# Window attention and two expert layers on one core: fifteen lists of steps in place of fixed offsets, key maxima two head pairs at once, and lists for the first steps of layer two

## The chip, the cores and the metric

The kernel runs on one core of a Trainium2 chip. The metric is the device time of one execution in microseconds (us), as the median of several runs. A core has five engines with a queue of instructions each: TensorE (PE; the loading of its weights is listed apart as PEld), VectorE (DVE), ScalarE (ACT), GpSimd (POOL) and SyncE (SP), which here only issues transfers (DMA). An engine runs its own queue in order and waits for others by semaphores.

## The reference, cut to what matters

```python
def _attn_ref(q, k, v):                       # 2 batches, 8 heads, 768 x 64
    block, window = (32, 16)
    k_sum = k.reshape(B, H, nb, block, D).max(axis=3)      # 24 key maxima
    v_sum = v.reshape(B, H, nb, block, D).mean(axis=3)     # 24 value means
    scores_l = scale * q @ k.T, kept where |i - j| < window
    scores_s = scale * q @ k_sum.T + log(block)
    a = softmax(concat([scores_l, scores_s]))   # with 1e-9 added to the sum
    return a @ concat([v, v_sum])

def _moe_ref(x, w_in, w_out, alpha):          # x 1536 x 512, w_in 512 x 2048, w_out 2048 x 512
    h = x @ w_in
    return (max(h, 0) + alpha * min(h, 0)) @ w_out

def _moe2_ref(x, w_in, w_out, a, b):          # the same sizes
    h = x @ w_in
    P = a[0] + a[1]*h + a[2]*h**2 + a[3]*h**3
    Q = 1 + abs(b[0])*abs(h) + abs(b[1])*h**2
    return (P / (Q + 1e-6)) @ w_out

def reference(...):
    x = _attn_ref(q, k, v), as 1536 x 512
    return _moe2_ref(_moe_ref(x, ...), ...)
```

## The kernel before, in words

**Attention.** The 1536 queries are 24 tiles of 64, n = 0 to 23; a tile has all eight heads, as four pairs. Its steps, by the names in the lists of orders and the lines of the functions: `qk`, the scores on PE into the one PSUM bank s (L554); `mask`, mask, scale and row minimum on DVE (L563); `sub`, for some tiles, subtracts the minimum ahead of the exponential; `exp` on ACT (L575, L579); `sum` on DVE (L584) or `guard` on one of three engines (L592 to L596), which form the sum d; `inv`, its reciprocal on DVE (L600); `norm`, p times d on POOL (L604); `turn`, a transpose on PE (L610); `turned`, the copy pT of it on ACT (L205); `pv`, the products po with the values (L624); `out`, a cast of po to xh (L205 on ACT, L207 on others); `outl`, the rest xl = po - xh on DVE (L645). The string SOFTMAX has one letter for each tile: a, the exponential sums itself by an accumulator and `guard` adds 1e-9; b, DVE sums; s, the minimum is subtracted first and one exponential does all four pairs. A tile's keys are copied to one of two buffers kc: `k` the strip of 96 keys for each pair, `ks` the 24 key maxima. The maxima (L477) are DVE reductions of one head pair and one half of a batch, eight for each batch. The value means are products on PE (`vmean`, L498; vps), for the second batch of rows that DVE has added in pairs (`vadd`, L493), copied out by ACT (L503) and put beside a tile's values by `vm`.

**Layer one beside it.** Every product with a weight is three products: weight and activation are each a high half of few bits and a low rest (xh and xl, wih and wil, woh and wol, g's two), and only low times low is left out. A weight arrives as raw 64-bit words in pieces of 1 MB, in two buffers. A piece is made ready in steps: ACT takes the tops (L230), DVE joins them to cv (`low`, L232), a cast gives the high half (`hi`), and two subtractions of 128x512 give the low one (`mid`, `end`, L253). For the first 512 tokens layer one begins as soon as their tiles are there: H (L290), the activation on DVE (`act`, L309 and L315), the cast of g and its low part (`gh`, `gl`, L207 and L354), Y (L370), in halves of 256 tokens for the first eight chunks of the hidden width. H and Y are numbered here in the order in which they come: 0 to 23 are the 24 of the first 512 tokens in layer one, and H24 and Y24 are the first of layer two.

**What sets the order.** There is no scheduler: each engine's order is the order in which the code issues. Iteration t = -1 to 27 walks one of seven lists in ORDERS, chosen by PHASES, and each step in it works on tile t plus a fixed offset. Ten constants (VMEAN_AT to WLOAD_AT) say at which iteration the loads, means and maxima come, BUSY and WARM where products of the unit matrix on itself are put whose result nobody reads ("idle", L674). The strings ENG name the engine of a step by phase: v is DVE, a is ACT, p is POOL.

**After attention** come what is left of layer one for the first 512 tokens (BETWEEN), the other 1024 tokens in a scheme that saves one product in eight (PAIRED, L920 and L941), and layer two (DECODE). There each round of `run` (its loop is below) issues an H, then the steps of the weights in preparation, the parts of P and Q of earlier chunks, up to six steps left over from PAIRED, and at most two Y.

Of the kernel before, what the change touches and what calls it, by code (L numbers as in the profile page):

```python
# [22 lines left out]
P = 128  # L23
WINDOW = 16
# [7 lines left out]
START_H = 6  # L32
N_FIRST = 3
HALVES = 8
EARLY = 8

VMEAN_AT = (-1, -1, 0, 1, 1, 2)
VADD_AT = (11, 11, 11)
VLOAD_AT = (9, 9, 9)
VSUM_AT = 12  # L40
KMAX_AT = (8, 9, 10, 8, 10, 10, 10, 10)
KLOAD_AT = (6, 8)
WLOAD_AT = (1, 3)

PHASES = (3, 5, 7, 10, 14, 20)
ORDERS = (
    "qk exp end sum k turn act vm vadd turned mask gh hi sub pv vmean kmax v gl in act new out H guard low inv "
    "mid Y ks act outl norm",
    "act hi exp low qk in mid vm turn mask gh sum act pv k H vmean turned gl out ks vadd guard act inv new v outl "
    "sub norm kmax Y end",  # L50
    "vm qk exp act mask mid pv v sum gh guard act Y kmax k out hi outl gl vadd low inv in norm ks turn end turned "
    "vmean H act sub new",
    "vm gh new act pv vadd exp mid hi end gl qk act act out kmax in sum outl turn k mask Y v vmean low guard sub "
    "ks inv turned norm H",
    "gh act end exp act ks qk mid gl act hi pv v out mask sum in outl Y vadd new sub vm vmean turn kmax H k "
    "turned guard inv low norm",
    "act act kmax act vm qk mask exp gh Y end guard sum gl pv vadd hi mid out k turn outl sub vmean H inv v norm "
    "ks new turned in low",
    "vm act exp hi qk vadd act act in guard mask k pv out kmax v outl sum gh Y mid turn new gl inv ks norm end H "
    "low vmean sub turned",  # L60
)

FIRST = 'v1 k0 v0 k1 v2 q0 v3 q1'

SOFTMAX = 'aaabbbaaaaasbbabaababbba'

ENG = {"vadd": "v", "guard": "pvavavaaaaa", "k": "vavaaapvaaa", "turned": "aaaaaaaaaaa", "vm": "pppvpvapaaa",
       "ks": "ppppvvvaaaa", "norm": "ppppppppaaa", "sub": "vpvvvpvaaaa", "gl": "vpppvpvvpvv", "gh": "aaapapavaap",
       "hi": "vvvaaaaaaav", "mid": "pvpppvvppvv", "end": "ppppppvvppp", "out": "aaavavaaaaa", "E1": "a",
       "neg": "aavvvvvvvvv", "th": "aaaavaaaaaa", "tl": "vvpppvpvppp", "ta": "p", "tb": "p",  # L70
# [7 lines left out]
LEAD = (5, 7, 3, 4, 13, 14, 9, 15)  # L78
CLOSE_E = 9
# [6 lines left out]
X_AT = (3, 4, 6)  # L86
# [11 lines left out]
BETWEEN, PAIRED, DECODE = 7, 8, 9  # L98
START_ORDER = ("new end Y P2 end P1 P6 E1 end T3 late P5 end ms C11 hi t11 low t11 l22 P7 T2 h21 low low P3 "
               "late U2 U4 U3 C22 hs new t22 t11 end low P4 new end C12 C21 t22 Y l21 t12 t21 T1 hi t12 ms es "  # L100
               "ms h22 hi t22 late mid ms t21 t12 Y mid low mid h11 es l11 h12 Y t21 T0 l12 end").split()
# [14 lines left out]
def kernel(  # L116
# [356 lines left out]
    def att_kmax(b, i):  # L473
        half, hp = divmod(i, NPAIR)
# [65 lines left out]
    def att_ksum(n):  # L540
        b, j = divmod(n, NSUB)
        if j < NKC:
            copy("ks", kc[n % NKC][:, :, STRIP:KEYS], kmax[b])

    def att_k(n):
        b, j = divmod(n, NSUB)
        half, j = divmod(j, HSUB)
        copy("k", kc[n % NKC][:, :, 0:STRIP], kt[b, half][:, :, j * QS:j * QS + STRIP])

    def att_scores(n):  # L550
        j = n % NSUB
        s = ps_s.tile([P, NPAIR, KEYS], F32, tag="s", name="s")
        for hp in range(NPAIR):
            nc.tensor.matmul(out=s[:, hp, :], lhsT=qz[n % NQZ][:, hp, :], rhs=kc[n % NKC][:, hp, :],  # L554
                             start=True, stop=True)
        st[n] = s
# [110 lines left out]
    def keep_busy(t, step):  # L667
        unread(BUSY.get((t, step), 0))

# [39 lines left out]
    later = {}  # L709

    acts, split_at = [], {}

    def ff_y(t):
        if split_at.get(y_list[0], t) < t and (0, "wo", y_list[0][1] // 2) in wts:
            y_mm(*y_list.pop(0))

    def ff_h(t):
        u, f = h_list[0]
        if u[:2] == (0, 0) and ready(u) <= t and (0, "wi", f // 2) in wts and len(y_list) - len(h_list) < 3:
            h_list.pop(0)  # L720
            h_mm(u, f)
            acts.append(act1(u, f))
            later[t + 2] = u, f
            split_at[u, f] = t + 2

    def vmean_at(t):
        for i, at in enumerate(VMEAN_AT):
            if at == t:
                att_vmean(i)
        while vlate:  # L730
            att_vload(vlate.pop(0))
        for i, at in enumerate(VLOAD_AT):
            if at == t:
                att_vpair(i)
        if t == VSUM_AT:
            att_vsum()

    def vadd_at(t):
        for i, at in enumerate(VADD_AT):
            if at == t:  # L740
                att_vadd(i)

    def kmax_at(t):
        for i, at in enumerate(KMAX_AT):
            if at == t:
                att_kmax(1, i)
# [14 lines left out]
    def w_step(place, most=0, alone=False):  # L761
# [5 lines left out]
        if len(w_now) < most and preps and preps[0] in raws and now[0] > loaded[preps[0]] + (1 if now[0] <= LAST else 2 if "wo" in kept and not rest and st2 else 0):  # L767
# [5 lines left out]
    attn = {"vm": (att_vm, -3), "ks": (att_ksum, 1), "k": (att_k, 1), "exp": (att_exp, -1), "qk": (att_scores, 0),  # L773
            "mask": (att_mask, 0), "sum": (att_sum, -1), "sub": (att_shift, 0),
            "guard": (att_guard, -1), "inv": (att_inv, -1), "norm": (att_norm, -1), "pv": (att_pv, -3),
# [4 lines left out]
    with tc.manual_schedule():  # L780
        for step in FIRST.split():
            {"k": lambda i: att_load(0, i), "v": att_vload, "q": att_in}[step[0]](int(step[1]))
        for i in range(2 * NPAIR):
            att_kmax(0, i)
# [339 lines left out]
```

## Time and profile before

| | before |
|---|---|
| median of 3 runs | 604.16 us (603.86 to 604.42) |
| profiled execution | 603.79 us |
| its span | 602.1 us |
| PE busy | 589.0 us, 98% |
| DVE busy | 518.6 us, 86% |
| ACT busy | 357.2 us, 59% |
| POOL busy | 304.6 us, 51% |
| moved by DMA | 71.64 MB, mean 119 GB/s |

The span runs from the first to the last instruction of the profiled execution; 1.7 us of its time lie around it. Busy times are of one execution. In the timeline an instruction has its start and its duration, and in brackets, where its engine sat idle ahead of it, for how long and what it waited for. Durations of PE's products overlap, since one product is still running out while the next is begun; where two follow each other without a pause, the distance of their starts is what one costs.

### The profile page before, as it was taken

The page shows a single profiled execution, that of the slowest core. Times are in us where ns is not written, and L with a number is a line of the kernel's source. Part 1 is how long each engine was busy: PE and PEld are TensorE (multiplying, and loading weights), DVE is VectorE, ACT ScalarE, POOL GpSimd, SP SyncE. Part 2 cuts the span into 40 slices and gives each one's busy share as a digit, 9 for nine tenths or more (in the row PEclk, how much of TensorE's full clock was granted, in tenths as well). Part 3 has the DMA queues.
Part 4 walks back from the last instruction along what each step waited for, and adds up shares of the span by engine and source line. Part 5 has one row for each costly group of instructions (what it writes and reads, how often), then busy time and mean ns, then how long its engine had stood idle before and what let it go on. Part 6 is the DMA issues. An engine that isn't in the chain of part 4 may idle for free.

```text
span 602.1 us, 9108 instructions
## 1 busy us (share of the span) xinstructions
PE 589.0 (98%) x3212; PEld 491.2 (82%) x3212; DVE 518.6 (86%) x990; ACT 357.2 (59%) x614; POOL 304.6 (51%) x332
## 2 busy tenths in 40 slices
PE   8998999999999999999999999999999999999997
PEld 6787899887888888888888778888888888888885
DVE  4689999989989999999988899999877778677785
ACT  1787778566465545554546878886555554454442
POOL 4475577686343424422442865456545554355552
PEclk9999999999999999999999999999999999999999
DMA  9999768424431342524334333330100000100001
GB/s 298 320 306 319 253 233 276 150 71 142 153 127 70 121 142 88 209 83 144 124 118 162 140 139 109 110 133 0 71 1 1 0 1 0 72 0 1 1 2 70
DMA packets 18862, 71.64 MB, mean 119 GB/s; under 512 B 2560, under 2 KB 4608, under 8 KB 12672
## 3 DMA queue, kind: packets, MB, share of 16 engines
q1 hardware_dynamic: 18816, 71.06, 34.5%
q8 instruction: 25, 0.41, 0.3%
q14 instruction: 21, 0.17, 0.1%
HBM read 67.91 MB, written 3.15 MB: 118 GB/s over the span
## 4 chain that ended last, share of the span: by engine, by line
PE 84%; DVE 9%; ACT 3%; POOL 2%; issue 2%; POOLq 0%; ACTq 0%; DVEq 0%
PE y L370 27%; PE h L290 26%; PE h L920 13%; PE h L941 7%; PE y L941 6%; DVE cv L232 2%; PE s L554 2%; PE vps L498 1%; PE po L624 1%; DVE wol L253 1%; ACT p L579 1%; PE pt L610 1%; DVE p L563 1%; ACT top L230 1%; DVE g L354 1%
## 5 line engine op out<-in xcount | busy, mean ns | idle before, releaser
L370 PE MATMUL y<-woh,g 128*128 128x512 f32 x384 | 126.2, 391 | 1.2 <-DVE g L354 1.2
L290 PE MATMUL h<-xh,wih 128*128 128x512 f32 (+1 forms) x288 | 106.9, 371 | 1.9 <-DVE tu L315 1.6
L290 PE MATMUL h<-xl,wih 128*128 128x512 f32 (+1 forms) x288 | 105.3, 366 | 0.8 <-DVE xl L645 0.8
L290 PE MATMUL h<-xh,wil 128*128 128x512 f32 (+1 forms) x288 | 105.2, 365 | 0.0
L329 POOL TENSOR_SCALAR tu<-tv,ab 128x512 f32<-128x512 f32 x48 | 38.8, 809 | 114.8 <-ACT tv L327 114.8
L370 PEld LDWEIGHTS y<-woh,g 128*128 128x128 f32 x384 | 71.7, 188 | 17.4 <-DVE g L354 2.7
L338 ACT ACTIVATE h<-tu,lnb 128x512 f32<-128x512 f32 x47 | 32.6, 693 | 82.7 <-DVE tp L332 80.3
L370 PE MATMUL y<-wol,g 128*128 128x512 f32 x192 | 74.7, 389 | 0.0
L230 ACT ACTIVATE top<-raw 128x1024 f16<-128x1024 bf16 x48 | 66.3, 1382 | 5.0 <-issue 2.5
L330 POOL TENSOR_TENSOR tu<-tu,tv 128x512 f32<-128x512 f32 x48 | 62.3, 1298 | 4.0
L290 PEld LDWEIGHTS h<-xh,wih 128*128 128x128 f32 x288 | 54.2, 188 | 11.4 <-DVE tu L315 2.1
L290 PEld LDWEIGHTS h<-xl,wih 128*128 128x128 f32 x288 | 54.3, 188 | 9.7 <-DVE xl L645 1.0
L232 DVE SCALAR_TENSOR_TENSOR cv<-raw,top 128x1024 int32<-128x1024 int32 x48 | 59.9, 1248 | 1.8 <-ACT top L230 1.6
L290 PEld LDWEIGHTS h<-xh,wil 128*128 128x128 f32 x288 | 54.2, 188 | 8.8
L340 DVE SCALAR_TENSOR_TENSOR tu<-tu,h 128x512 f32<-128x512 f32 x47 | 32.2, 686 | 28.2 <-ACT h L339 28.0
L205 ACT ACTIVATE wih<-cv 128x1024 fp32r<-128x1024 f32 x31 | 32.5, 1052 | 27.4 <-DVE cv L232 27.4
L604 POOL TENSOR_TENSOR p<-p,d 128x480 f32<-128x480 f32 x24 | 31.2, 1301 | 32.2 <-DVE d L600 26.8
L997 DVE TENSOR_TENSOR e<-h,e 128x512 f32<-128x512 f32 x56 | 37.8, 688 | 9.4 <-PE h L920 7.5
L370 PE MATMUL y<-g,woh 128*128 128x256 f32 (+1 forms) x192 | 45.5, 328 | 0.2 <-DVE g L354 0.2
L1023 POOL TENSOR_TENSOR g<-tu,g 128x512 fp32r<-128x512 f32 x16 | 28.3, 1768 | 29.7 <-ACT g L205 29.0
L370 PEld LDWEIGHTS y<-wol,g 128*128 128x128 f32 x192 | 36.0, 188 | 7.6
L354 DVE TENSOR_TENSOR g<-tp,g 128x512 fp32r<-128x512 f32 (+1 forms) x55 | 38.3, 696 | 1.8 <-POOL g L207 1.6
(141 smaller groups left out, 1419.2 us busy)
## 6 DMA issues: line engine op xcount, KB each, us to landing
raw<-in_w_in SPq DMA_DIRECT2D x24, 1024.0 KB, 4.8
raw<-in_w_out SPq DMA_DIRECT2D x24, 1024.0 KB, 4.7
qz<-in_qT SPq DMA_DIRECT2D x24, 256.0 KB, 4.9
vc<-in_vS SPq DMA_DIRECT2D x24, 192.0 KB, 5.0
kt<-in_kT SPq DMA_DIRECT2D x16, 208.0 KB, 5.5
out<-stage SPq DMA_DIRECT2D x12, 256.0 KB, 2.3
vt<-in_vS SPq DMA_DIRECT2D x6, 256.0 KB, 4.4
vp<-in_vS SPq DMA_DIRECT2D x3, 512.0 KB, 8.0
```

The source lines that it names most:

```text
L205: e.activation(out=out, in_=in_, func=AF.Copy, scale=1.0 if scale is None else scale)
L230: nc.scalar.activation(out=top.bitcast(F16)[:, 1::2], in_=raw.bitcast(BF16)[:, 4:4100:4], func=AF.Copy)
L232: nc.vector.scalar_tensor_tensor(out=w.bitcast(I32), in0=rest, scalar=13, in1=top, op0=ALU.logical_shift_right, op1=ALU.bitwise_or)
L290: nc.tensor.matmul(out=ps, lhsT=a, rhs=b, start=(c == 0 and m == 0), stop=(c == NC - 1 and m == 2))
L329: nc.gpsimd.tensor_scalar(out=q, in0=v, scalar1=ab[:, 1:2], scalar2=ab[:, 0:1], op0=ALU.mult, op1=ALU.add)
L330: nc.gpsimd.tensor_tensor(out=q, in0=q, in1=v, op=ALU.mult)
L338: nc.scalar.activation(out=A, in_=q, func=AF.Ln, scale=2.0 ** -LN_SHIFT, bias=lnb)
L354: (eng("gl") if (u, f) != steps[-1] else nc.vector).tensor_tensor(out=gl, in0=t, in1=gh.bitcast(F32), op=ALU.subtract)
L370: nc.tensor.matmul(out=yps[c][:, c0:c0 + n] if layer == 0 else yps[c], lhsT=a, rhs=b, start=(f == 0 and c0 == 0 and m == 0), stop=(f == NF ...
L920: nc.tensor.matmul(out=ps, lhsT=a[:, cs], rhs=b, start=c == 0 and m == 0, stop=c == 1 and m == 2)
L941: nc.tensor.matmul(out=ps, lhsT=a[:, f, cs], rhs=g[:, b, :], start=f == 0 and m == 0 and (tile == 2 or j == 0), stop=f == 1 and m == 2 and ...
L997: nc.vector.tensor_tensor(out=sums[out], in0=a, in1=sums[b], op=ALU.add)
```

## The change

**The first fifteen iterations** (t = -1 to 13) get a list each, EARLY_ORDERS. A step has no offset any more: a counter for each kind of step says which tile is next, so that one iteration may do a step twice or not at all. The loads, means, maxima and additions of the constants are steps in these lists too (`M`, `K`, `kload`, `kmax`, `vload`, `vadd`, `vsum`, `wload`), and so are the idle products (`z4` is four). Two lists of ORDERS remain, for t = 14 to 19 and from 20 on. The strings of ENG have an entry for nearly every early iteration. SOFTMAX has other letters, and the first loads have another order.

**The second batch's key maxima** are four reductions of two head pairs, 128x2x12, in place of eight of 128x12.

**Layer two** is issued by a new loop, `decode`, with one list for each of its first fourteen rounds and a common one behind. The orders of PAIRED (START_ORDER, PAIR_ORDER, REST_ORDER) are sorted anew in part.

Branches for `DIRECT` and for a `norm` on DVE or ACT are written too, with DIRECT = 0 and with every `norm` on POOL.

The diff, cut to its core (of the lists only some rows):

```diff
-PHASES = (3, 5, 7, 10, 14, 20)
+PHASES = (0, 1, 2, 3, 4, 5, 6, 7, 8, 9, 10, 12, 14, 20)
+EARLY_ORDERS = (
+    "K z4 mid hi K K hi end K in K M k low K K K",
...
+    "qk mid exp sum v low mid vm pv turn in mask z1 k turned hi wload ks out guard new inv outl v norm vm",
...
+    "low norm mid gh pv gl act v qk hi out in end Y mask sum ks k new vm vsum sub guard turn H outl turned inv "
+    "norm low new",
+)
-SOFTMAX = 'aaabbbaaaaasbbabaababbba'
+SOFTMAX = 'abaabaaabaasbsbbaabaaaba'
...
-        nc.vector.tensor_reduce(
-            out=kmax[b][:, hp, half * NB // 2:(half + 1) * NB // 2],
-            in_=kt[b, half][:, hp, WINDOW:WINDOW + S // 2].rearrange("p (n i) -> p n i", i=BLOCK),
+            out=kmax[b][:, hp:hp + n, half * NB // 2:(half + 1) * NB // 2],
+            in_=kt[b, half][:, hp:hp + n, WINDOW:WINDOW + S // 2].rearrange("p h (n i) -> p h n i", i=BLOCK),
...
+    def attention(x):
+        n = done[x]
+        if n >= limit.get(x, NQ):
+            return
...
+        step_of[x](n)
+        done[x] += 1
...
+    def decode():
...
+        first = s
+        while y_list:
+            k = s - first
...
+            for x in (DECODE_FIRST[k] if k < len(DECODE_FIRST) else DECODE_ORDER).split():
+                if x == "H":
+                    if h_list and (h_list[0][0][0], "wi", h_list[0][1] // 2) in wts:
+                        u, f = h_list.pop(0)
+                        h_mm(u, f)
+                        chain["p"][0].append((u, f, s))
+                elif x in chain:
+                    due, fn, then = chain[x]
+                    if due and (k < len(DECODE_FIRST) or x == "gl" or due[0][2] < s):
...
+                elif x == "Y":
...
-        run(lambda: y_list)
+        decode()
```

What this makes of the engines' queues is shown at three places. A name such as p3_193 is a buffer (p3, the fourth of the four p) with its number in the program; numbers and lines differ between the two kernels.

POOL, from the norm of tile 3 to the first weights of layer one. Before:

```order
L604 TENSOR_TENSOR p3_193<-p3_193,d_366 128x4x120
L604 TENSOR_TENSOR p0_190<-p0_190,d_421 128x4x120
L799 TENSOR_SCALAR al1_78<-al_77 128x16
L253 TENSOR_TENSOR wil_479<-cv_386,wih_478 128x512
L604 TENSOR_TENSOR p1_191<-p1_191,d_462 128x4x120
L253 TENSOR_TENSOR wil_479<-cv_386,wih_478 128x512
L604 TENSOR_TENSOR p2_192<-p2_192,d_514 128x4x120
L207 CAST g_632<-tu_562 128x256
L253 TENSOR_TENSOR wil_578<-cv_492,wih_577 128x512 x2
L354 TENSOR_TENSOR g_632<-tu_562,g_632 128x256
L604 TENSOR_TENSOR p3_193<-p3_193,d_602 128x4x120
L207 CAST g_705<-tp_634 128x256
```

and after, with the first half of w_out at the end:

```order
L624 TENSOR_TENSOR d_365<-ds3_201 128x4
L634 TENSOR_TENSOR p3_193<-p3_193,d_365 128x4x120
L229 COPY kc0_174<-kt_217 128x4x96
L634 TENSOR_TENSOR p0_190<-p0_190,d_415 128x4x120
L831 TENSOR_SCALAR al1_78<-al_77 128x16
L229 COPY kc1_175<-kt_217 128x4x96
L634 TENSOR_TENSOR p1_191<-p1_191,d_451 128x4x120
L624 TENSOR_TENSOR d_493<-ds2_200 128x4
L634 TENSOR_TENSOR p2_192<-p2_192,d_493 128x4x120
L275 TENSOR_TENSOR wil_567<-cv_486,wih_566 128x512
L376 TENSOR_TENSOR g_644<-tu_555,g_644 128x256
L275 TENSOR_TENSOR wil_567<-cv_486,wih_566 128x512
```

The two copies of keys have come to POOL, two additions of d too; the first weight's two low halves (wil_479) and the cast of the first g (g_632) have gone.

DVE at the same place, from the last mask of tile 6 to the first activation (tu). Before:

```order
L584 TENSOR_REDUCE d_462<-p1_191 128x4
L207 COPY kc1_175<-kt_217 128x4x96
L645 TENSOR_TENSOR xl_89<-po_516,xh_88 128x4x64
L232 SCALAR_TENSOR_TENSOR cv_492<-raw_391,top_86 128x1024
L600 RECIPROCAL d_462<-d_462 128x4
L309 TENSOR_SCALAR tu_562<-h_547,al_77 128x256
```

and after:

```order
L275 TENSOR_TENSOR wil_470<-cv_375,wih_469 128x512
L682 TENSOR_TENSOR xl_89<-po_509,xh_88 128x4x64
L254 SCALAR_TENSOR_TENSOR cv_486<-raw_371,top_86 128x1024
L628 RECIPROCAL d_451<-d_451 128x4
L275 TENSOR_TENSOR wil_470<-cv_375,wih_469 128x512
L331 TENSOR_SCALAR tu_555<-h_542,al_77 128x256
```

The sum of tile 5 and the copy of keys have gone; both low halves of the first weight stand there in their place.

PE at the passage into layer two: the end of an H, and the Y or H behind it (h_3821 and h_3814 are H27 in both; woh and wol are the two halves of layer two's first piece of w_out, y0 to y3 its four banks of sums). Before:

```order
L290 MATMUL h_3821<-xh_2423,wih_3127 128x512
L290 MATMUL h_3821<-xl_2424,wih_3127 128x512
L290 MATMUL h_3821<-xh_2423,wil_3128 128x512
L370 MATMUL y0_3857<-woh_3471,g_3837 128x512
L370 MATMUL y0_3857<-wol_3472,g_3837 128x512
L370 MATMUL y0_3857<-woh_3471,g_3837 128x512
L370 MATMUL y1_3861<-woh_3471,g_3837 128x512
L370 MATMUL y1_3861<-wol_3472,g_3837 128x512
L370 MATMUL y1_3861<-woh_3471,g_3837 128x512
```

and after:

```order
L312 MATMUL h_3814<-xh_2415,wih_3287 128x512
L312 MATMUL h_3814<-xl_2416,wih_3287 128x512
L312 MATMUL h_3814<-xh_2415,wil_3288 128x512
L312 MATMUL h_3833<-xh_2415,wih_3622 128x512
L312 MATMUL h_3833<-xl_2416,wih_3622 128x512
L312 MATMUL h_3833<-xh_2415,wil_3623 128x512
L312 MATMUL h_3833<-xh_2415,wih_3622 128x512
L312 MATMUL h_3833<-xl_2416,wih_3622 128x512
L312 MATMUL h_3833<-xh_2415,wil_3623 128x512
```

Before, Y24 follows; after, H28 stands there, and Y24 and Y25 behind it.

## Rows read from the trace of the kernel before

**Rows 1.** The page's first lines: the span, and PE's busy time and instructions

```profile
span 602.1 us, 9108 instructions
...
PE 589.0 (98%) x3212; PEld 491.2 (82%) x3212; DVE 518.6 (86%) x990; ACT 357.2 (59%) x614; POOL 304.6 (51%) x332
```

**Rows 2.** Stretches from:to: length, busy us of each engine, PE clock, DMA share, GB/s

```profile
15.00:45.00 30.00, 27.85 (x284) 23.47 (x283) 22.13 (x103) 25.11 (x73) 16.88 (x21) 1.00 0.96 314
45.00:75.00 30.00, 27.48 (x252) 23.92 (x249) 27.28 (x92) 21.81 (x59) 17.85 (x16) 1.00 0.89 285
...
90.00:150.00 60.00, 59.10 (x498) 51.71 (x498) 56.57 (x156) 39.65 (x87) 45.11 (x48) 1.00 0.48 162
```

**Rows 3.** Timeline of PE: start, duration, instruction, idle time before and its releaser

```profile
29.24 1.15 PE L554 MATMUL s<-kc,qz 128*128 128x120 f32 x8 [0.43 <-DVE kc L207]
...
33.35 0.39 PE L290 MATMUL h<-xl,wih 128*128 128x256 f32 x1 [0.80 <-DVE xl L645]
...
39.24 0.69 PE L624 MATMUL po<-pT,vc 120*64 120x64 f32 x16 [0.52 <-ACT pT L205]
...
46.33 0.39 PE L370 MATMUL y<-g,wol 128*128 128x256 f32 x1 [0.64 <-POOL wol L253]
...
54.98 0.39 PE L290 MATMUL h<-xh,wih 128*128 128x256 f32 x1 [1.20 <-DVE tu L315]
...
63.14 0.65 PE L610 MATMUL pt<-ident,p 128*120 128x128 f32 x4 [0.67 <-ACT vmean L503]
```

**Rows 4.** Timeline of DVE, tiles 3 and 5: sums, copy of keys, xl

```profile
26.00 0.65 DVE L584 TENSOR_REDUCE d<-p 128x4 f32<-128x484 f32 x1
...
31.88 0.66 DVE L584 TENSOR_REDUCE d<-p 128x4 f32<-128x484 f32 x1 [0.45 <-ACT p L579]
32.45 0.50 DVE L207 COPY kc<-kt 128x384 f32<-128x384 f32 x1
32.88 0.41 DVE L645 TENSOR_TENSOR xl<-po,xh 128x256 fp32r<-128x256 f32 x1
```

**Rows 5.** Timeline of POOL: copies, addition of d, norm of tile 3, g

```profile
10.35 0.66 POOL L207 COPY kc<-kmax 128x96 f32<-128x96 f32 x2 [2.73 <-DVE kmax L477]
14.57 0.20 POOL L596 TENSOR_TENSOR d<-ds 128x4 f32<-128x4 f32 x1 [3.56 <-ACT p L579]
...
27.03 0.99 POOL L604 TENSOR_TENSOR p<-p,d 128x480 f32<-128x480 f32 x1 [2.84 <-DVE d L600]
...
40.16 0.40 POOL L207 CAST g<-tu 128x256 fp32r<-128x256 f32 x1
```

**Rows 6.** Timeline of ACT: first exponential of tile 7

```profile
39.09 0.39 ACT L579 ACTIVATE p<-p,m 128x120 f32<-128x120 f32 x1
```

**Rows 7.** Low halves: timelines of POOL and DVE, then durations on DVE (L253)

```profile
76.42 1.29 POOL L253 TENSOR_TENSOR wol<-cv,woh 128x512 fp32r<-128x512 f32 x1
...
76.97 1.29 DVE L253 TENSOR_TENSOR wil<-cv,wih 128x512 fp32r<-128x512 f32 x1
...
L253 DVE TENSOR_TENSOR wil<-cv,wih x50: 655/684/1346, 77.0 to 400.1; 128x512 fp32r<-128x512 f32 x50
```

**Rows 8.** Timeline of DVE: key maxima of the second batch and their copy

```profile
50.10 2.38 DVE L477 TENSOR_REDUCE kmax<-kt 128x12 f32<-128x384 f32 x5
...
53.99 0.60 DVE L207 COPY kc<-kmax 128x96 f32<-128x96 f32 x1
```

**Rows 9.** Passage to layer two: timeline of PE, then of DVE

```profile
345.46 0.39 PE L370 MATMUL y<-woh,g 128*128 128x512 f32 x1
...
347.26 0.73 PE L370 MATMUL y<-woh,g 128*128 128x512 f32 x2 [1.19 <-DVE g L354]
...
352.39 0.39 PE L370 MATMUL y<-woh,g 128*128 128x512 f32 x1
...
346.52 0.69 DVE L354 TENSOR_TENSOR g<-tp,g 128x512 fp32r<-128x512 f32 x1
...
351.22 0.68 DVE L354 TENSOR_TENSOR g<-tp,g 128x512 fp32r<-128x512 f32 x1
```

More of the change, by code (lines that the diff above doesn't have):

```diff
@@ L29 @@
 LN_SHIFT = 64
-START_H = 6
+START_H = 4
 N_FIRST = 3
@@ L35 @@
 EARLY = 8
[L37 to L43, printed above, removed]
-PHASES = (3, 5, 7, 10, 14, 20)
-ORDERS = (
[L47 to L60, printed above, removed]
-)
@@ L63 @@
-FIRST = 'v1 k0 v0 k1 v2 q0 v3 q1'
-SOFTMAX = 'aaabbbaaaaasbbabaababbba'
[L67 to L70, printed above, removed]
+DIRECT = 0
@@ L85 @@
 PAIR = 2
-X_AT = (3, 4, 6)
+X_AT = (4, 5, 6)
 PAUSE = 3
@@ L547, in att_k @@
         half, j = divmod(j, HSUB)
-        copy("k", kc[n % NKC][:, :, 0:STRIP], kt[b, half][:, :, j * QS:j * QS + STRIP])
+        if n >= DIRECT:
+            copy("k", kc[n % NKC][:, :, 0:STRIP], kt[b, half][:, :, j * QS:j * QS + STRIP])
     def att_scores(n):
@@ L708 @@
     loads = list(preps)
[L709 to L746, printed above, removed]
+    h_at, split_at = {}, {}
     w_now = []
@@ L778 @@
-    every = {"Y": ff_y, "H": ff_h, "vmean": vmean_at, "vadd": vadd_at, "kmax": kmax_at}
+    step_of = {"vm": att_vm, "ks": att_ksum, "k": att_k, "exp": att_exp, "qk": att_scores, "mask": att_mask, "sum": att_sum,
+               "sub": att_shift, "guard": att_guard, "inv": att_inv, "norm": att_norm, "pv": att_pv, "turn": att_turn, "out": att_out,
+               "outl": att_outl, "turned": att_turned, "in": att_in, "v": att_v, "M": att_vmean, "K": lambda i: att_kmax(0, i, 1),
+               "kload": lambda i: att_load(1, i), "kmax": lambda i: att_kmax(1, i, 2), "vload": att_vpair, "vadd": att_vadd,
+               "vsum": lambda i: att_vsum(), "wload": lambda i: w_load(*loads.pop(0))}
@@ new lines @@
+    done = defaultdict(int, {"in": 2})
+    def attention(x):
+        n = done[x]
+        if n >= limit.get(x, NQ):
+            return
+        assert all(done[y] > n - back for y, back in after.get(x, ()) if n >= back), (x, n)
+        if x == "pv" and n % NSUB < NVC:
+            assert done["vm"] > n
+        if x == "ks" and n % NSUB < NKC + DIRECT:
+            assert (done["kmax"] == NPAIR if n >= NSUB else done["K"] == 2 * NPAIR)
+        if x == "k" and n >= NSUB:
+            assert done["kload"] > (n - NSUB) // HSUB
+        if x == "kmax":
+            assert done["kload"] > 2 * n // NPAIR
+        if x == "vm":
+            assert done["vsum"] if n >= NSUB else done["M"] == NV
+        if x == "vadd":
+            assert done["vload"] > n
+        if x == "vsum":
+            assert done["vadd"] == NV // 2 and done["turn"] == done["turned"]
+        step_of[x](n)
+        done[x] += 1
+        if x == "M":
+            while vlate:
+                att_vload(vlate.pop(0))
@@ L780, with next_act @@
+    act, to_split, to_low = [], [], []
+    def next_act():
+        if act and next(act[0][0], 0) == 0:
+            to_split.append(act.pop(0)[1])
     with tc.manual_schedule():
@@ L782 @@
             {"k": lambda i: att_load(0, i), "v": att_vload, "q": att_in}[step[0]](int(step[1]))
-        for i in range(2 * NPAIR):
-            att_kmax(0, i)
-        unread(WARM)
         for t in range(-1, LAST + 1):
```

178 lines of the change are left out of this document (117 added, 61 removed), and 14 rows, old and new, of the table DECODE_FIRST.

## The prediction, made before the changed kernel had run

> **What bounds the kernel now.** I read the head of the page first, then TensorE by stretches of time, then its named waits, and last the queues of the engines that it waits for. TensorE (PE) is busy 589.0 of 602.1 us, so only the other 13.1 us, and the unread "idle" products inside the 589.0, can be won without taking out arithmetic [rows 1]. The change takes out none: PE's products are as many as before, and so are the dummies, in other places. The table by stretches says where idle time is: 2.15 us in 15 to 45 us, 2.52 in 45 to 75, 0.90 in 90 to 150 [rows 2]; another 1.19 is one wait at 347.26, in the passage to layer two [rows 9]. So it is the first iterations, the pieces of layer one beside the second batch, and that passage that can move the end. The named waits fit: 0.43 us of the scores of tile 6 for a copy of keys, 0.80 of the first H for xl, 0.52 of po of tile 5 for the copy pT, 0.64 of the first Y for half a weight, 1.20 of an H for VectorE's tu, 0.67 of a transpose for vmean [rows 3]. VectorE (DVE) is the fullest engine beside PE, 27.28 of 30 us in 45 to 75 and 56.57 of 60 in 90 to 150; ScalarE (ACT) has 25.11 of 30 in 15 to 45 [rows 2].
>
> **The change, part by part.** The sum is made against the profiled execution, 603.79 us, which is its span of 602.1 and 1.7 around it; it lies 0.37 below the median, 604.16.
>
> *First iterations, 15 to 45 us.* Four waits in PE's order, one behind the other, so that what each loses adds up.
> The 0.43: the copy kc of these tiles is on DVE, behind the sums (0.50 and 0.66 a tile later, at 32.45 and 31.88) [rows 4]. In after it is on POOL, right behind the norm of tile 3. That norm loses the DVE sum of 0.65 at 26.00 ahead of it (tile 3's exponentials now sum themselves) and gets an add on POOL of 0.20 instead, so it starts 0.45 earlier than 27.03 and ends at 27.6 instead of 28.0 [rows 4, 5]. What a 128x384 copy costs on POOL no row shows; the copy of 128x96 takes 0.33 (0.66 for two), four times that is 1.3 [rows 5]. It would end between 27.9 and 28.9, and the scores that wait for it begin at 29.24 now. Gain 0.3 to 0.43; I take 0.43, since the copies of two tiles leave DVE.
> The 0.80: the last xl of the first four tiles stands on DVE at 32.88, behind that kc copy and a sum that waited 0.45 for ACT [rows 4]. Sum and copy go; half a weight, 0.68 in the median of its kind [rows 7], comes in their place. From 31.43, where DVE began to wait, that puts xl at 32.1, 0.77 earlier. I take the whole 0.80.
> The 0.52: pT on ACT stands behind casts and copies; two casts of xh come to ACT there, one kc copy goes. I take half, 0.26.
> The 0.64: on POOL two casts of g, 0.40 each as the one at 40.16, stand ahead of the half of w_out that Y waits for [rows 5]. One moves to ACT, the other behind that half: 0.8 off, so the 0.64 goes.
> Sum A = 2.1. Two things hide work here: DVE takes both halves of the first w_in while POOL normalizes, and ACT takes the cast of it. What it costs if that cover is gone is the first two rivals' matter.
>
> *45 to 75 us.* The 0.67 goes: the products of the second batch's means, and so vmean, move from behind y2 to behind y3, past one more Y. The loads for them stand on SP behind one more raw weight of 1.05 MB, 3.3 us at 314 GB/s [rows 2]; a Y and what goes with it takes PE about as long, so I take it as covered, and if it is not, the 0.67 stays. The 1.20 I leave nearly whole. Before the tu that H waits for DVE has five reductions of keys, 2.38 us together, and the copy kc<-kmax of 0.60 [rows 8]. In after, three of the four double reductions stand there. No row shows a double one; it lies between one single (0.48) and two (0.95). At 0.95 three are 2.86, 0.48 more than now; the copy of 0.60 goes to ACT. That leaves 0.12 to win; at 0.48 it would be 1.5, more than the wait. I take 0.95, since the number of elements is twice as large and nothing in the rows says that a part of 0.48 is paid once. B = 0.67 + 0.12 = 0.8, between 0.1 and 1.9.
>
> *90 to 150 us.* Three halves of weights go from DVE to POOL, two casts of g from POOL to ACT. A half takes 0.68 on DVE in the median and 1.29 on POOL [rows 7]; DVE is at 56.57 of 60 and loses 2.0, POOL at 45.11 gains 3.9 and loses 0.8 [rows 2]. PE's idle time there, 0.90, is the ceiling; I take C = 0.8, and 0 as the other end.
>
> *Into layer two.* Y24 begins at 345.46 and stops for g, whose low part DVE computes from 346.52 [rows 9]. In after the H that stood behind Y24 stands ahead of it, and fills the pause. Both are done at 352.39 now, at 351.2 without the wait of 1.19. Y25, which comes next in after, wants its own g, which DVE computes from 351.22 and has at 351.9 [rows 9]. So Y25 can begin at 351.9 instead of 352.39: D = 0.5, between 0 and 1.2 (DVE earlier too).
>
> *Priced at nothing.* The branches for a constant DIRECT = 0 and for a norm on ACT or DVE are not reached: all 24 norms stay on POOL. The dummies cost PE the same in sum. PE's granted clock is 1.00 in every stretch [rows 2]; of the dummies ahead of the first scores six move behind them, which should leave it there. [...]
>
> *Sum.* 2.1 + 0.8 + 0.8 + 0.5 = 4.2 off a span of 602.1 gives 597.9, 599.6 with what lies around it, and 0.37 more for the median: **600.0 us**.
>
> **A rule against the change.** At 76.97 half a weight takes 1.29 us on DVE, beside one of 1.29 on POOL that began at 76.42; the median on DVE is 0.68 [rows 7]. So two such subtractions at once cost DVE about 0.6. [...]
>
> **The rivals.**
> *The halves stop each other (R1).* Each moved half stops DVE by 0.6. C is then 0 (three halves free 2.0 of DVE and stop it 1.9). The two first halves on DVE run beside POOL's work at 1.29 [rows 7]: 1.2 off A, which leaves 0.9. B without the 0.12 is 0.7, D stays 0.5. Sum 2.1: 602.1 us. For it speaks the row at 76.97; against it the median of 0.68 while POOL is more than half busy.
> *ACT as a link in the chain (R2), slower.* In after ACT has, ahead of the exponentials of tile 7, the casts xh of tiles 4 and 5. Now these exponentials begin at 39.09, and po of tile 5 only at 39.24, for 0.69 [rows 3, 6]. If po5 ends where it does now, the cast (0.4) pushes the exponentials to 40.3, 1.2 late, and with them the norm, the transpose of tile 7 and the first Y behind it. Further on the copy kc<-kmax stands on ACT behind DVE's last reduction and holds the next pT: 0.6, its time on DVE [rows 8]. With ACT late the casts of g that come to it cost C, and the gains of A and B are gone: +1.2 + 0.6 - 0.5 = +1.3, 605.5 us. It decides from po5 ending later than 38.7 (39.09 less the cast). Against it: the first two terms of A put po5's end at 39.93 - 1.23 = 38.7, and half of the 0.52 makes it 38.4, clear by a little only.
> *All waits go (R3).* The double reductions cost about one single and ACT keeps up: 2.15 + 2.52 + 0.90 + 1.19 = 6.8, 597.4 us; a little more if the queue of loads, busy 0.96 of 15 to 45 [rows 2], brings the weights in a better order.
> *Nothing moves (R4).* The same products in nearly the same order, with the waits only renamed: 604.2.
>
> **How the numbers follow.** Forecast 0.46, 598.3 to 601.8; R1 0.20, 601.3 to 603.4; R3 0.14, 596.2 to 598.2; R2 0.13, 604.8 to 606.3; R4 0.07. The time is the likeliest's, 600.0. The range that leaves out most of R2 and the lowest end of R3 is 596.5 to 604.6. A measurement of this kernel can tell about 0.2%, 1.2 us, from no change: faster is under 602.95. That is the forecast, R3 and four fifths of R1, less a little for waits that I have not seen, 0.74; slower is most of R2, 0.12; the rest, 0.14, is the same.
>
> **What would show it.** A: the first product of Y with wol, at 46.33 now, begins near 44.2, and neither it nor the first H waits; were it still at 46, R1 or R2. R2: po5 ends after 38.7 and the exponentials of tile 7 wait for xh. B: how long a double reduction takes, and whether the H behind it waits. C: PE's idle time in the sixty microseconds around the last tiles, and halves on DVE at 0.68 or 1.29. D: Y24 without a wait, Y25 with one of about 0.7. If PE has a new gap between 150 and 320, or a clock under 1.00 in the first 30 us, the whole sum is wrong.

## The result and the profile after

The changed kernel takes 607.20 us (median of 4 runs, 607.03 to 608.45) against 604.22 for the kernel before: ratio 1.0054, interval 1.0037 to 1.0072. It is 0.5% slower, 7.2 us above the forecast of 600.0 and outside its range. The page's first lines after, to be held against [rows 1]:

```profile
span 605.5 us, 9094 instructions
...
PE 590.7 (98%) x3212; PEld 490.8 (81%) x3212; DVE 510.5 (84%) x971; ACT 358.6 (59%) x627; POOL 307.1 (51%) x336
```

PE has the same number of instructions, DVE has become freer by 8 us, ACT and POOL are busier by 1.4 and 2.5, and the span is 3.4 us longer. To find where, I took the start of the same step on PE in both traces and subtracted (after minus before, us). A column falls where the changed kernel wins time and rises where it loses:

| step on PE (its start before) | after | e4 | e8 |
|---|---|---|---|
| scores of tile 0 (11.2) | +1.86 | +0.15 | +0.42 |
| scores of tile 11 (52.3) | +2.23 | +0.88 | +0.88 |
| scores of tile 14 (70.1) | +4.69 | -0.01 | -0.03 |
| scores of tile 18 (89.8) | +5.00 | +0.31 | +0.27 |
| ahead of the paired stage (152) | +3.04 | -1.65 | -1.68 |
| its last product (343) | +3.46 | -1.27 | -1.68 |
| H29 (355) | +2.72 | -2.02 | -1.63 |
| H32 (372) | +3.41 | -1.29 | -1.72 |
| last product (598) | +3.40 | -1.25 | -1.65 |

(e4 and e8 are experiments below.) So the loss is 1.86 before the first scores, 0.37 in the first tiles, 2.46 between tiles 11 and 14, 0.31 up to tile 18; 1.96 is won from there to the end of attention, 0.42 lost in the paired stage, and layer two changes nothing. The forecast had neither the first nor the third of these.

**Before the first scores.** The timeline of PE, before:

```profile
1.59 5.73 PE L674 MATMUL idle<-ident 128*128 128x128 f32 x26 [1.59 <-POOL ident masks.py:199]
7.64 1.88 PE L498 MATMUL vps<-vt,mean 128*24 128x512 f32 x4 [0.32 <-POOL mean L456]
9.45 1.93 PE L674 MATMUL idle<-ident 128*128 128x128 f32 x12
11.22 1.09 PE L554 MATMUL s<-kc,qz 128*128 128x120 f32 x8
```

and after:

```profile
1.59 2.07 PE L708 MATMUL idle<-ident 128*128 128x128 f32 x8 [1.59 <-POOL ident masks.py:199]
7.26 3.61 PE L520 MATMUL vps<-vt,mean 128*24 128x512 f32 x4 [3.59 <-POOL mean L478]
10.80 2.44 PE L708 MATMUL idle<-ident 128*128 128x128 f32 x18
13.08 1.05 PE L583 MATMUL s<-kc,qz 128*128 128x120 f32 x8
```

Four passes of the value means took 1.88 us where 26 passes of dummies stood ahead of them, and 3.61 where eight passes and 3.59 us of idleness did: half the speed. Behind them stand nine dummies (two passes each) of 2.4 us, six before, and only behind those the scores, whose keys are copied at 10.8.

The records of PE's granted clock have two values in both traces, 1.00 and 0.50. After, the products of the H at 58.16 begin 0.12 us apart from 58.38 to 58.97, at 1.00, and 0.21 apart from 59.18 to 60.03, at 0.50. At the start the column says nothing: the trace's first record of the clock, at 1.00, begins at 6.54 us before and at 11.17 after, and ahead of it the column shows 1.00 for want of a record. The dummies' own passes tell the level. In both traces they begin 0.21 us apart ahead of that record, and behind it 0.11 but for the first of a group. So PE starts at the lower level; before, it came to the upper one among the first 26 passes, at 6.54, and after, only when the means were done, at 11.17.

**Between tiles 11 and 14.** PE's waits after, named as in [rows 3] and [rows 9]:

```profile
35.02 0.38 PE L312 MATMUL h<-xh,wih 128*128 128x256 f32 x1 [0.50 <-ACT xh L227]
...
48.22 0.39 PE L392 MATMUL y<-g,wol 128*128 128x256 f32 x1 [0.32 <-POOL wol L275]
...
58.16 0.39 PE L312 MATMUL h<-xh,wih 128*128 128x256 f32 x1 [2.15 <-DVE tu L337]
...
72.81 0.65 PE L647 MATMUL pt<-ident,p 128*120 128x128 f32 x4 [0.67 <-ACT vmean L525]
...
355.41 0.73 PE L392 MATMUL y<-woh,g 128*128 128x512 f32 x2 [0.43 <-DVE g L376]
...
367.19 0.73 PE L392 MATMUL y<-woh,g 128*128 128x512 f32 x2 [0.35 <-DVE g L376]
```

The wait of the H for tu, 1.20 before, is 2.15. What DVE does ahead of that tu:

```profile
52.97 1.79 DVE L499 TENSOR_REDUCE kmax<-kt 128x24 f32<-128x768 f32 x2
...
54.91 2.34 DVE L254 SCALAR_TENSOR_TENSOR cv<-raw,top 128x1024 int32<-128x1024 int32 x1
...
57.68 0.42 DVE L337 SCALAR_TENSOR_TENSOR tu<-h,tu 128x256 f32<-128x256 f32 x1
```

and POOL beside it:

```profile
53.65 2.52 POOL L275 TENSOR_TENSOR wol<-cv,woh 128x512 fp32r<-128x512 f32 x2
56.13 1.97 POOL L634 TENSOR_TENSOR p<-p,d 128x480 f32<-128x480 f32 x1
```

The joining cv took 2.34 where it takes 1.22 in the median of this kernel, and the norm on POOL 1.97 where the median is 0.99: it looks as if each stands in the other's way (e1 and e9 bear on it). The wait has a second price, as the stretches show (length, busy us of PE, PEld, DVE, ACT and POOL, PE's granted clock, DMA share, GB/s):

```profile
56.00:58.00 2.00, 0.00 (x1) 0.00 (x0) 1.97 (x3) 0.69 (x2) 2.00 (x2) 1.00 1.00 383
58.00:60.00 2.00, 1.84 (x11) 1.84 (x12) 0.91 (x9) 0.61 (x3) 2.00 (x3) 0.74 1.02 360
60.00:62.00 2.00, 2.00 (x21) 1.66 (x20) 1.51 (x4) 0.99 (x2) 0.90 (x2) 0.50 1.06 424
62.00:64.00 2.00, 2.00 (x17) 2.00 (x17) 2.00 (x11) 0.00 (x0) 0.88 (x2) 0.91 1.03 426
```

PE was idle for all of 56 to 58, and behind that its granted clock is 0.50, the lower of the two values, from 58.96 to 62.37 us. Of the 2.46 us lost here 0.95 are the longer wait and 1.5 are products at that clock: in e2, an experiment below, the wait is 2.14 and the clock stays at 1.00, and the same steps lose 0.97. In e9, a later one, the clock stays at 1.00 behind a wait of 2.97.

### The profile page after: what moved, and what is told of

Its sections match the earlier page's. It is cut to its first block, busy times and chain, and to the rows that moved or that the text cites. A ratio compares the mean times of both kernels' runs of the same rounds, so it can differ in the third digit from the quotient of the medians.

```text
span 605.5 us, 9094 instructions
## 1 busy us (share of the span) xinstructions
PE 590.7 (98%) x3212; PEld 490.8 (81%) x3212; DVE 510.5 (84%) x971; ACT 358.6 (59%) x627; POOL 307.1 (51%) x336
## 4 chain that ended last, share of the span: by engine, by line
PE 90%; DVE 4%; ACT 3%; issue 1%; POOL 1%; POOLq 0%; DVEq 0%; ACTq 0%
PE y L392 27%; PE h L312 27%; PE h L985 13%; PE h L1006 7%; PE y L1006 7%; PE s L583 3%; PE po L661 2%; PE pt L647 2%; PE vps L520 2%; ACT p L607 1%; DVE cv L254 1%; ACT top L252 1%; PE idle L708 1%; DVE p L591 1%; DVE tp L364 0%
## 5 line engine op out<-in xcount | busy, mean ns | idle before, releaser
L254 DVE SCALAR_TENSOR_TENSOR cv<-raw,top 128x1024 int32<-128x1024 int32 x48 | 62.9, 1310 | 3.0 <-ACT top L252 2.8
L1088 POOL TENSOR_TENSOR g<-tu,g 128x512 fp32r<-128x512 f32 x16 | 30.0, 1878 | 29.5 <-ACT g L227 28.8
```

The lines of the kernel that those rows point to most:

```text
L254: nc.vector.scalar_tensor_tensor(out=w.bitcast(I32), in0=rest, scalar=13, in1=top, op0=ALU.logical_shift_right, op1=ALU.bitwise_or)
```

## The experiments

In each comparison the kernel before ran on the same chip, at 604.4 to 604.6; the changed kernel's 607.20 is from the first one, where it was 604.22.

**e1, the dummies ahead of the first scores as before.**

```diff
-    "K z4 mid hi K K hi end K in K M k low K K K",
-    "ks end M z9 new qk mask k sub in new exp M v",
+    "K z13 mid hi K K hi end K in K M k low K K K",
+    "ks end M z6 new qk mask k sub in new exp M v",
```

> The changed kernel with the idle products ahead of the first scores as in the kernel before: 13 ahead of the first two value means (instead of 4) and 6 behind them (instead of 9). Theory 'cold start': after 3.59 us of idleness the two value means ran at 0.89 us a product pass instead of 0.45, and nine dummies stood before the scores; with TensorE busy up to them the scores of tile 0 begin near 11.2 instead of 13.1 and all that follows is 1.8 earlier: about 605.4 against 607.2. Rival 'loads': the first tiles wait for loads anyway, the 1.8 is lost again before the first Y (its start stays near 47.4), and the time stays within 0.5 of 607.2.

Measured 604.82 us (603.22 to 606.06, 11 runs), 2.4 less than the changed kernel. The timeline of PE:

```profile
7.26 1.90 PE L520 MATMUL vps<-vt,mean 128*24 128x512 f32 x4 [1.08 <-POOL mean L478]
9.09 1.60 PE L708 MATMUL idle<-ident 128*128 128x128 f32 x12
11.38 0.79 PE L583 MATMUL s<-kc,qz 128*128 128x120 f32 x5 [0.69 <-DMA qz<-in_qT]
```

The means are back at 1.90 and the scores at 11.4. The gain is still 1.59 at tile 11, so the rival (loads) falls. The theory's reason has to be put otherwise: PE had not fallen to the lower clock in its 3.59 us of idleness, it had not yet left it. Here the first record of the upper one is at 4.59, among the dummies.

In the profiled run the clock stayed at 1.00 and the H waited for tu 1.00 instead of 2.15; this run, 603.22, is the fastest of the eleven. With the same order on both engines it was POOL that was held up this time, DVE and then POOL:

```profile
53.28 1.23 DVE L254 SCALAR_TENSOR_TENSOR cv<-raw,top 128x1024 int32<-128x1024 int32 x1
52.04 3.60 POOL L275 TENSOR_TENSOR wol<-cv,woh 128x512 fp32r<-128x512 f32 x2
```

The halves took 3.60 instead of 2.52, and cv 1.23 instead of 2.34. In four of the other runs the mean granted clock was 0.996 or 0.997 as in the changed kernel, and these are the ones at 605.3 to 606.1.

**e2, without the nine dummies between the means and the first scores.**

```diff
-    "ks end M z9 new qk mask k sub in new exp M v",
+    "ks end M new qk mask k sub in new exp M v",
```

> The changed kernel without the nine idle products that stand between the first two value means and the first scores. If the nine alone set the start: scores of tile 0 near 10.8 (the keys are copied at 10.8), 2.2 earlier, total about 605.0. If the slow value means are what counts, and TensorE is still slow behind them: the scores of tile 0 take about twice their 1.0 us, so that 1 us of the 2.2 is lost again, about 606.2.

Measured 606.02 us (604.09 to 607.23, 11 runs), 1.2 more than e1; in the profiled runs the H behind tile 11 waits 2.14 here and 1.00 there. The timeline of PE:

```profile
7.26 3.61 PE L520 MATMUL vps<-vt,mean 128*24 128x512 f32 x4 [3.59 <-POOL mean L478]
...
11.48 1.12 PE L583 MATMUL s<-kc,qz 128*128 128x120 f32 x8 [0.61 <-DMA qz<-in_qT]
```

The means are as slow as in the changed kernel, and the scores begin at 11.5 all the same and are not slow; they wait here for their queries, not for PE. The slow means alone end at 10.8, when the keys come, and cost nothing. So the loss takes both, slow means and dummies behind them: e1 takes the one away, e2 the other, and either brings 1.6 to 1.7 of the 1.86 back. Nine dummies behind fast means would cost nothing either, by an estimate from e1: six more passes at 0.11 would end at 11.4, when the queries come. The time lies at the other theory's figure, 606.2, but for another reason, the wait of the H.

**e3, the two parts of tu ahead of cv on DVE.**

```diff
-    ... exp k new H low act",
+    ... exp k new H act act act low",
```

> The changed kernel with the two parts of the fourth activation (tu) on VectorE ahead of the joining of the next weight (cv, 2.34 us at 54.91 in the changed kernel) instead of behind it. Theory: the H at 58.16 waits 2.15 only for this order on VectorE, and TensorE's granted clock falls to 0.50 in 58.5 to 62 only because it was idle then; with tu done near 55.9 the wait goes to under 0.3, the clock stays at 1.00, and 2.2 + 1.5 = 3.7 are won: about 603.5. Rival: cv, now 0.9 later, is what the next weight and its H or Y wait for: the wait moves, and the time stays above 606.

Measured 604.64 us (603.96 to 605.73, 11 runs), 2.6 less than the changed kernel. The stretches where the changed kernel stood still:

```profile
56.00:58.00 2.00, 2.00 (x20) 2.00 (x18) 1.97 (x3) 1.44 (x6) 2.00 (x2) 1.00 1.05 377
58.00:60.00 2.00, 1.94 (x27) 1.67 (x27) 2.00 (x12) 0.01 (x1) 2.00 (x3) 1.00 1.00 385
60.00:62.00 2.00, 2.00 (x18) 1.77 (x16) 2.00 (x6) 0.90 (x3) 2.00 (x2) 1.00 1.07 428
```

The wait is gone and the clock is 1.00 from its first record, at 12.72, to the end. It is less than the 3.7 expected, since in the profiled run the scores of tile 0 began 0.74 later still than in the changed kernel: the clock came up 1.55 later, and the eighteen passes of dummies took 3.19 instead of 2.44. From there on the gain is 3.3. The rival, that cv is then late for something else, falls.

**e4, both.** 

> Both edits together, the idle products as in the kernel before and tu ahead of cv. If both theories hold and their places are independent: 1.8 + 3.7 off, about 601.7, below the kernel before (604.2). If one covers the other (a start 1.8 earlier meets the same loads or the same cv): between 603 and 605.

Measured 602.37 us (601.86 to 602.53), ratio to before 0.9959 (0.9946 to 0.9973): faster than the kernel before, and 4.8 below the changed one. The two gains, 2.4 and 2.6, add up but for 0.2, and with both edits the changed kernel is faster than the one before.

**e5, e4 without the 24 dummies behind the first scores** (all later z steps taken out of the lists).

> The kernel of e4 (602.4) without the 24 idle products that stand behind the first scores (each two passes of 0.112 us, 5.4 us in all). If they stand where TensorE would have waited anyway, the waits come out in the profile in their place and the time stays at 602.4 within 0.5, or the clock falls there and it is 604 or more. If they cost what they take, the first Y comes several us earlier and the time is 598 to 600.

Measured 603.50 us (601.27 to 604.09, 11 runs), 1.1 more than e4. The waits come out where the dummies stood; the longest, on PE:

```profile
27.18 1.60 PE L583 MATMUL s<-kc,qz 128*128 128x120 f32 x8 [2.48 <-ACT kc L227]
...
34.84 0.39 PE L312 MATMUL h<-xh,wih 128*128 128x256 f32 x1 [1.70 <-ACT xh L227]
```

and the clock goes with them (stretches as above):

```profile
25.00:30.00 5.00, 2.82 (x25) 2.50 (x26) 3.55 (x20) 4.48 (x16) 1.63 (x3) 0.77 0.96 324
30.00:35.00 5.00, 3.30 (x33) 2.88 (x32) 2.80 (x14) 4.00 (x13) 1.61 (x3) 0.89 1.04 295
```

Both releasers are ACT. So the dummies cover real waits for ACT. But what their absence costs is the clock: the two runs with a mean clock of 0.999 took 601.27 and 601.74, less than any run of e4, and the nine with 0.993 to 0.997 took 602.20 to 604.09. Neither of the two outcomes expected is the whole. As far as these runs tell, the dummies cost 0.6 to 1.1 us (601.74 and 601.27 against e4's median) and spare more than that by keeping the clock up.

**e6, e4 with every double reduction as two single ones.**

```diff
-"kmax": lambda i: att_kmax(1, i, 2)
+"kmax": lambda i: (att_kmax(1, 2 * i, 1), att_kmax(1, 2 * i + 1, 1))
```

> The kernel of e4 with each double reduction of key maxima done as two single ones at the same place. The double one took 0.94 us (0.90 each in a pair) where a single one takes 0.48. Theory: the time goes by elements, so this changes nothing: 602.4 within 0.4. Rival: the double ones save a fixed part, and this is 0.5 or more slower, with a wait of the H behind them.

Measured 602.41 us (602.35 to 603.37), the same as e4. A double reduction costs two single ones; this part of the change is worth nothing either way.

**e7, e4 with the first low half of every weight from iteration 20 on back on DVE** (one letter of ENG["mid"] from p to v).

> The kernel of e4 with the first of the two low halves of every weight from iteration 20 on back on VectorE, as it was in the kernel before (the changed kernel has it on GpSimd). Theory: the 1.2 to 1.9 us that the changed kernel wins between 110 and 150 us come from this relief of VectorE; undone, TensorE waits for g and tp there again (0.9 us in the kernel before), and the time is 603.3 to 604.2. Rival: the halves on GpSimd stop VectorE for as long as they relieve it, and undoing it changes nothing, 602.4 within 0.4.

Measured 604.98 us (604.43 to 605.21, 11 runs), 2.6 more than e4, which is more than the 1.2 to 1.9 I expected. PE waits again:

```profile
108.96 0.39 PE L312 MATMUL h<-xh,wih 128*128 128x256 f32 x1 [0.35 <-DVE tp L337]
115.60 0.39 PE L312 MATMUL h<-xh,wih 128*128 128x256 f32 x1 [1.38 <-DVE tu L337]
```

So the gain behind tile 18 is this move. How the halves stand without it and with it, by groups of 90 to 150 us (count, busy us, mean ns). On DVE before:

```profile
L253 DVE TENSOR_TENSOR wil<-cv,wih 128x512 fp32r<-128x512 f32 x7 | 5.6, 796 | 0.0
L253 DVE TENSOR_TENSOR wol<-cv,woh 128x512 fp32r<-128x512 f32 x5 | 5.6, 1112 | 1.1 <-ACT woh L205 1.1
```

and after, on DVE, then on POOL:

```profile
L275 DVE TENSOR_TENSOR wil<-cv,wih 128x512 fp32r<-128x512 f32 x4 | 2.7, 682 | 0.0
...
L275 DVE TENSOR_TENSOR wol<-cv,woh 128x512 fp32r<-128x512 f32 x2 | 1.4, 681 | 0.0
...
L275 POOL TENSOR_TENSOR wol<-cv,woh 128x512 fp32r<-128x512 f32 x4 | 5.3, 1334 | 0.3 <-ACT woh L227 0.3
L275 POOL TENSOR_TENSOR wil<-cv,wih 128x512 fp32r<-128x512 f32 x4 | 5.2, 1288 | 0.0
```

Twelve halves of 11.2 us on DVE have become six of 4.1, and two on POOL have become eight: six have moved, and those that stay on DVE are no longer stretched either.

**e8, e4 with the second part of the change undone** (loop, orders of the paired stage, order of preparing weights).

```diff
-        decode()
+        run(lambda: y_list)
```

> The kernel of e4 with the second part of the change undone: the loop, the orders of the paired stage, and the order of preparing weights as in the kernel before. By the starts of TensorE's products this part lost 0.4 us in the paired stage, won 0.7 at the passage into layer two and lost it again 12 us later: 602.0 within 0.4. Rival: the new lists are worth the 0.5 that was predicted, and undone the time is 602.9 or more.

Measured 602.00 us (601.85 to 602.14), ratio 0.9961 (0.9948 to 0.9973). In the table its column is at -1.68 at 152 us and at -1.65 at the end, where that of e4 goes from -1.65 to -1.25. The old wait is there as in [rows 9]:

```profile
345.59 0.74 PE L392 MATMUL y<-woh,g 128*128 128x512 f32 x2 [1.20 <-DVE g L376]
```

and costs no more than what stands in its place after. The new lists for layer two are worth nothing, and the new orders of the paired stage lose about 0.4. That rests on the starts in three traces (0.42 lost after, 0.38 in e4, nothing in e8); the times of e4 and e8, 602.37 and 602.00, differ by less than their intervals. Which of the moves loses it, PE's rows don't tell: no wait is named there.

**e9, the changed kernel with the two low halves of iterations 10 and 11 on DVE** (a letter each of ENG["mid"] and ENG["end"] from p to v).

> The changed kernel itself (607.2), with the two low halves of w_out of iterations 10 and 11, which GpSimd computes in 2.52 us from 53.65, on VectorE as two of 0.68. Theory 'the engines stop each other': the joining cv at 54.91 took 2.34 us instead of its median 1.22 only because GpSimd's two-input operations run beside it; with them gone cv takes 1.2 to 1.7 (the norm stays beside it), VectorE gives back the 1.36 of the halves for it, and the wait of the H at 58.16 stays between 1.5 and 2.6: 606.5 to 607.5. Rival: cv is long for another reason (its own input, a load); then it stays at 2.3, the wait grows to 3.5 and the time to 608.5 or more.

Measured 608.79 us (608.40 to 609.76). On DVE:

```profile
53.10 0.69 DVE L275 TENSOR_TENSOR wol<-cv,woh 128x512 fp32r<-128x512 f32 x1 [2.55 <-POOL woh L229]
...
57.51 1.20 DVE L254 SCALAR_TENSOR_TENSOR cv<-raw,top 128x1024 int32<-128x1024 int32 x1
```

and on PE:

```profile
55.85 0.39 PE L312 MATMUL h<-xl,wih 128*128 128x256 f32 x1 [2.97 <-DVE xl L682]
```

On cv the theory was right: without POOL's halves beside it, it takes 1.20 instead of 2.34. But e1 had 1.23 with the halves beside it, so two traces alone don't prove the cause: in the changed kernel DVE was held up (cv 2.34, the two halves 2.52), in e1 POOL (1.23 and 3.60). On the time the theory was wrong, and the rival's figure is nearer, for a reason that neither had: the first half now stands on DVE behind a cast of woh that POOL does, DVE waits 2.55 for it, and an H behind it 2.97 for xl. The six halves left on DVE behind tile 18 take 0.68 each: in the trace of after none of them overlaps one of POOL's eight.

**e10, e8 with the first queries loaded earlier.**

```diff
-FIRST = 'v0 v1 k0 k1 v2 q0 v3 q1'
+FIRST = 'v0 v1 k0 k1 q0 v2 q1 v3'
```

> The kernel of e8 (602.0) with the first queries loaded ahead of the third and fourth rows of values. In e4 and e8 the first scores wait 0.6 to 0.7 us for these queries. Theory: the start is what all else follows; the scores begin 0.5 to 0.6 earlier (near 10.9, when the keys are copied), 601.4. Rival: the value means behind the first scores now wait for their rows, or the keys come no earlier, and it stays at 602.0 within 0.3.

Measured 601.25 us (601.18 to 602.11), ratio 0.9950 (0.9938 to 0.9963). The scores of tile 0 begin 0.92 earlier than in e8, and in the profiled runs 0.96 is left at the end. In the medians it is 0.75, and one of the five runs, 602.11, lies among those of e8.

**e11, e8 with the H ahead of the transpose that waits for vmean.**

```diff
-    ... vm vsum sub guard turn H outl turned inv "
+    ... vm vsum sub guard H turn outl turned inv "
```

> The kernel of e8 (602.0) with the H that follows the transpose behind the second batch's value means put ahead of that transpose. The transpose waits 0.67 us for vmean wherever the means stand, since both use the one PSUM bank pt, from which ACT must first copy the means out. Theory: that copy is hidden behind the H, the 0.67 is won: 601.3. Rival: the H isn't ready that early, or the softmax of the next tile, whose transpose is now 1.5 later, becomes the wait: 602.0 or more.

Measured 601.76 us (601.32 to 601.81). The wait of 0.67 is gone, and the scores of tile 14 begin 0.66 earlier than in e8. The runs of e8 and e11 don't overlap, but their difference, 0.24, is smaller than either's interval, so only the removal of the wait is shown.

**e12, e10 and e11 together.** 

> The edits of e10 and e11 together. If both hold: 600.8, 0.6 per cent under the kernel before. If only one does, 601.3 to 601.5.

Measured 600.90 us (600.57 to 601.88), ratio 0.9941 (0.9927 to 0.9954): the lowest median of all, though not clear of e10's, 0.6% below the kernel before and 1.0% below the changed one.

## Why the prediction was wrong, point by point

**The start was not looked at.** This is the step that failed first: the part "Priced at nothing" says that the dummies cost PE the same in sum, and that moving six of them behind the first scores should leave the clock at 1.00. Their number is the same, but nine of them no longer stand ahead of the value means, where with their eighteen passes the clock had come up in time (at 6.54 before, at 11.17 after). The means ran at the lower level (3.61 us instead of 1.88), nine dummies stood between them and the first scores, which are on the path of all that follows, and the start came 1.86 later (e1 and e2 each take most of it away). My table of stretches began at 15 us; it could not show it. The sign that I gave for it, a clock under 1.00 in the first 30 us, held up to 11.17, though the column could not show that either. The lower clock stood in the trace of before to be read: the dummies are 0.21 us apart up to 6.54 and 0.11 from there on.

**First iterations, -2.1 forecast, +0.37 measured.** The waits changed in part as told: the 0.43 and the 0.52 are gone, the 0.64 is 0.32, and the 0.80 has become 0.50 for another input, xh of ACT; new ones of 0.4 and 0.3 came. All PE's time from the scores of tile 0 to those of tile 11 (stretches as above), before and after:

```profile
11.22:52.29 41.07, 38.08 (x366) 31.85 (x365) 30.68 (x139) 33.68 (x103) 22.41 (x26) 1.00 0.96 309
```

```profile
13.08:54.52 41.44, 39.55 (x378) 33.17 (x377) 30.70 (x131) 33.68 (x108) 23.91 (x29) 1.00 0.90 289
```

PE's idle time fell from 2.99 to 1.89, half of what I forecast, and its busy time rose by 1.47, with twelve products more: behind the first scores 48 passes of dummies stand after and 36 before, some 1.3 us more. So the six dummies moved behind the first scores were paid for here, which is the same step again. A named wait that goes is no gain where dummies are issued in its place; e5 shows that beneath them PE waits up to 2.48 us for ACT. The rival R2 had the right engine, and its link is there too. The timeline of ACT after, xh of tile 5 and the first exponential of tile 7:

```profile
41.72 0.38 ACT L227 ACTIVATE xh<-po 128x256 fp32r<-128x256 f32 x1 [1.37 <-PE po L661]
42.00 0.39 ACT L607 ACTIVATE p<-p,m 128x120 f32<-128x120 f32 x1
```

ACT sits idle 1.37 us for po5, and the exponentials begin 2.91 later than in [rows 6], 1.05 more than the start explains. The first product of Y with wol, at 48.22 or 46.36 without the start, stands where I had said that it would speak for R1 or R2. But the price that R2 put on it is not seen: the scores of tile 10, behind the first Y, are 1.88 later than before, which is the start's 1.86.

**45 to 75 us, -0.8 forecast, +2.46 measured.** The size of a double reduction was right (0.95 taken, 0.94 measured; e6). Wrong was the term beside it: I carried cv at what it took before, 1.20, and it took 2.34, so that the wait I left at 1.08 became 2.15 (with cv at 1.23, in e1, it was 1.00). Rival R1 had this mechanism, but I put its price on the halves alone and on another place; here it fell on the DVE instruction between the maxima and tu. The second half of the loss, 1.5 at the lower clock behind a wait of 2.15, was in no rival. And the 0.67 did not go: it moved from 63.14 to 72.81 with the means, because the transpose behind them needs the bank that ACT must first empty, wherever they stand. e11 hides it behind an H. The 0.31 lost from there to tile 18 was not followed.

**90 to 150 us, -0.8 forecast, -1.96 measured.** Mechanism right (e7), size wrong. I had counted three halves, and six moved. And I had made PE's named idle time, 0.90, the ceiling; it went to nothing, but the same 510 products between the scores of tile 18 and the paired stage also take 60.55 us of busy time instead of 61.61, so PE was being held up by 1.06 without a wait being named. The halves that stay on DVE became shorter too. R1, which gave 0 here, falls for this stretch.

**Into layer two, -0.5 forecast, 0 measured.** Up to H29 the step is right: against the stretch ahead of it that H comes 0.74 earlier, and Y25 waits 0.43 (the row at 355.41). The row at 367.19 shows what I did not follow further: the second Y behind it waits 0.35 for its own g. DVE's chain of g's looks like the limit there, since a pause filled at one place opens at the next and e8, with the old pause of 1.20, ends no later.

**The paired stage, 0 forecast, +0.42 measured.** I did not price its sorted orders at all; e8's trace shows the loss, its cause is open.

## What to carry to other kernels

Trace an edit from the first instruction on: what stands ahead of the first product on the critical path is paid in full (1.86 us here), and filler work there is as dear as real work. Filler where the engine would stand idle anyway was free here, and with it the clock came up sooner (at 4.59 in e1, at 11.17 in the changed kernel); moved behind, it cost its time and the clock. A wait of the critical engine is priced with what it waits for at the durations that the new neighbours give (cv took 2.34 here, 1.22 in the median), and, where the clock has fallen behind it, with the products there at the lower clock (1.5 us here). A wait that goes counts only after the next one behind it on the releasing engine has been looked at.

## What the runs showed of the hardware that I had not expected

In before, after, e1 to e4, e8 and e9 PE began at the lower clock: the first 8 passes of dummies took 2.07 or 2.08 us, the first 26, where there were so many, 4.59 to 5.73, and twelve behind the means of e1 1.60. When the clock came up differed between runs of the same early code: at 11.17 us in the changed kernel, 12.72 in e3 and 10.07 in e9, which share all their early dummies, and the first scores began at 13.08, 13.82 and 12.58. Where 26 passes of dummies stood ahead of the means it came up at 4.59 (e1) and 6.54 (before). The profile's clock column shows 1.00 ahead of its first record, so at the start the level is to be read from the distance of like products (0.21 and 0.11 us for the dummies here).

Behind a wait of 2.15 at 56 us the clock did fall, to 0.50, and in e5 behind one of 2.48 at 25 (a mean of 0.77 in 25 to 30 us). In e2 a wait of 2.14 at the same H left it at 1.00 in the profiled run, while four other runs of e2 had a mean clock of 0.996 or 0.997; in e9 one of 2.97 left it at 1.00. Whether the clock falls is not settled by the length of the wait alone, and what settles it stays open.
